# Four neighbouring rows per partition: another order of the rows of q, k and v, and of the output

## The chip, the cores and the metric

The kernel runs on one core of a Trainium2 chip. The metric is the device time of one execution in microseconds, the median of three runs. Five engines work in parallel, each through its own queue in order: PE (matrix multiply), DVE (vector), ACT (activation), POOL (GpSimd) and SP, which here issues nearly all transfers (DMAs). A time with "profile" beside it is from one further execution, recorded by the profiler.

## The reference

Attention over 8 batches of 8 heads, 576 rows and 64 columns, where each query keeps only its 32 largest scores, followed by two matrix products with a squared ReLU between them:

```
scores = (q @ k.T) / 8                      # 576 x 576 for each head
kth    = 32nd largest score of each row
scores = where(scores >= kth, scores, -1e9)
attn   = softmax(scores)
x      = (attn @ v), heads side by side     # 4608 x 512
out    = square(relu(x @ w_in)) @ w_out     # 512 -> 2048 -> 512, float32
```

## The kernel before

**The work.** Two heads form a pair, and a pair is loaded together (`load_pair`, from line 653; for the first pair `load_first`, from line 597). The 576 rows of a head are taken as four blocks of 128 and a rest of 64. The tiles `rq` and `rk` have the shape 128 x 5 x 2 x 64 (partition, block, head, column), so a partition holds the same row of both heads side by side; `rv` has 128 x 10 x 64, with the four blocks of one head after another and then the two rests. For one head of q or k one DMA brings the four blocks (line 663, 128 KB) and one the rests of both heads (line 666, 32 KB); v has two DMAs of 128 KB (line 673) and two of 16 KB (line 677). Before the change, block `tb` holds rows `128*tb` to `128*tb + 127`, so a partition's four rows lie 128 rows apart in DRAM.

PE transposes the blocks (line 585), ACT copies them into `qk` (lines 711 to 714), POOL casts v into `vb` (line 715; line 647 for the first pair). A group is one block of 128 queries of a pair: PE computes its scores against all 576 keys of both heads into PSUM (line 582), ACT copies them to `s` (line 755), DVE and POOL find the 32nd largest. For this the 576 columns are folded as four quarters of 144 (DVE line 905, POOL line 900): the largest of each four in one list, the others in three more, and then eight are taken at a time with MAX8 and MATCH_REPLACE8 (lines 934 to 946). This is right only if each list yields no more than it should; `verdict` (line 1388) tests it at the end of the kernel, and if a row failed, the whole work is done again by a second plan that runs MAX8 over all 576 columns. Four groups are searched by a threshold instead (`hunt`, with a MAX8 at line 814), and have a test of their own. ACT turns the threshold into a mask (line 965), PE transposes and masks the scores, ACT takes the exponential (line 1021), and PE multiplies by v.

**The output side.** POOL divides (line 1096), a DMA transposes `x` into `xt` (line 1109; line 1115 for the rests), and `feed` (from line 1121) runs the two matrix products over chunks of 128 or 256 rows. ACT copies each result of 128 rows to `o` (two buffers, line 1172), and SP stores it (line 1180): 128 rows of 2 KB, next to each other in the output. The last 128 rows go through `feed_last` (from line 1184), which stores two halves of 256 columns (line 1245).

**The order.** A planner (`Plan.schedule`, line 141) simulates the five queues when the kernel is built. Each operation has a duration, a priority and the tiles that it takes; the planner writes the order of each queue from that, and the order is then fixed. Where it sees PE idle it adds matmuls on `ones_bf` or `ident_bf` that compute nothing needed; ten of them stand at the start. Loads are planned by the number of their DMAs and a bandwidth figure, not by their patterns. The SP queue is in order too: a DMA that waits for its buffer holds the ones behind it. The first pair's k comes by three DMAs: one head and the rests on ACT's queue, the other head on SP's; the first block of q comes before the other three.

Of the kernel before, what the change touches and what calls it, by code (L numbers as in the profile page):

```python
# [13 lines left out]
P = 128  # L14
# [370 lines left out]
def bass_top_k_attn__then__act_relu_squared_kernel(  # L385
# [8 lines left out]
    NB, H, S, D = q.shape  # L394
# [194 lines left out]
    def build(full, weights, pl):  # L589
# [7 lines left out]
        def load_first(b, hp, rq, rq2, rk, base):  # L597

            def part(t, src, h, tb, n_):
                r0 = 128 * tb + (64 if h and src is k else 0)  # L600
                return at(t)[:, tb:tb + n_, h, :], src[b, 2 * hp + h, r0:r0 + 128 * n_, :].rearrange(
                    "(tb p) d -> p tb d", p=P)

            def rest(t, src, r0, d0):
                x = src[b, 2 * hp, r0:r0 + 64, :]
                return at(t)[0:64, 4, :, :], bass.AP(x.tensor, x.offset, [x.ap[0], [(S + d0) * D, 2], x.ap[1]])

            def start(queue, *parts):
                return lambda: [queue.dma_start(*x()) for x in parts]

            both = bass.AP(q.tensor, q[b, 2 * hp, 0:P, :].offset, [[D, P], [S * D, 2], [1, D]])
            pl.op("sp", .1, base - 82, start(nc.scalar, lambda: part(rk, k, 0, 0, 4),
                                             lambda: rest(rk, k, REST[0], REST[1] - REST[0])),
                  w=[rk], take=[rk], sem=slot_sem, ndma=2, via="act")
            pl.op("sp", 4.0, base - 81, start(nc.sync, lambda: part(rk, k, 1, 0, 4)), w=[rk], sem=lambda o: "first", ndma=1)
            pl.op("sp", 3.5, base - 80, start(nc.sync, lambda: (at(rq)[:, 0, :, :], both)), w=[rq], take=[rq],
                  sem=slot_sem, ndma=1)
            pl.op("sp", 3.5, base - 79, start(
                nc.sync, lambda: part(rq2, q, 0, 1, 3), lambda: part(rq2, q, 1, 1, 3), lambda: rest(rq2, q, 512, 0)),
                w=[rq2], take=[rq2], sem=slot_sem, ndma=3)  # L620
# [32 lines left out]
        def load_pair(b, hp, base):  # L653
            rq, rk, rv = tile("rq"), tile("rk"), tile("rv")


            def load(t, src, rest):
                def fn():
                    r = at(t)
                    res = []  # L660
                    for h in range(2):
                        r0 = 64 if h and rest != (512, 512) else 0
                        res.append(nc.sync.dma_start(r[:, 0:4, h, :], src[b, 2 * hp + h, r0:r0 + 512, :].rearrange(
                            "(tb p) d -> p tb d", p=P)))
                    x = src[b, 2 * hp, rest[0]:rest[0] + 64, :]
                    res.append(nc.sync.dma_start(r[0:64, 4, :, :], bass.AP(
                        x.tensor, x.offset, [x.ap[0], [(S + rest[1] - rest[0]) * D, 2], x.ap[1]])))
                    return res
                return fn

            def loadv():
                r = at(rv)
                res = [nc.sync.dma_start(r[:, 4 * h:4 * h + 4, :], v[b, 2 * hp + h, 64 * h:64 * h + 512, :].rearrange(
                    "(tb p) d -> p tb d", p=P)) for h in range(2)]

                for h in range(2):
                    res.append(nc.sync.dma_start(r[64 * h:64 * h + 64, 8 + h, :], v[b, 2 * hp + h, REST[h]:REST[h] + 64, :]))
                return res

            via = not full and not state["pairs"]  # L680
            state["pairs"] += 1
            if via:
                rq2 = tile("rq")
                load_first(b, hp, rq, rq2, rk, base)
            else:
                pl.op("sp", 2.3, base - 80, load(rq, q, (512, 512)), w=[rq], take=[rq], sem=slot_sem, ndma=3,
                      bw=BW * 1.9)
                pl.op("sp", 2.3, base - 79.9, load(rk, k, REST), w=[rk], take=[rk], sem=slot_sem, ndma=3, bw=BW * 1.9)
            pl.op("sp", 2.3, base - 70, loadv, w=[rv], take=[rv], sem=slot_sem, ndma=4, bw=BW * 1.9)
            qk, vb = tile("qk"), tile("vb")  # L690
            if via:
                return first_pair(rq, rq2, rk, rv, qk, vb, base)
            tq, tk, tx = Tile(psum), Tile(psum), Tile(psum)

            def t4(o, src):
                def fn():
                    for tb in range(4):
                        ins = tr(bank(o)[:, 128 * tb:128 * tb + 128], at(src)[:, tb, :, :].rearrange("p h d -> p (h d)"), ident32[:, :])
                    return ins
                return fn  # L700

            def t5():
                for i, s in enumerate((rq, rk)):
                    ins = tr(bank(tx)[:, 64 * i:64 * i + 64], at(s)[0:64, 4, :, :].rearrange("p h d -> p (h d)"), ident32[0:64, 0:64])
                return ins

            o_q = pl.op("pe", .46, base - 45, t4(tq, rq), r=[rq], w=[tq], take=[tq, qk])
            pl.op("pe", .49, base - 44.9, t4(tk, rk), r=[rk], w=[tk], take=[tk], order=[o_q])
            pl.op("pe", .22, base - 44.8, t5, r=[rq, rk], w=[tx], take=[tx], order=[o_q])

            pl.op("act", .565, base - 42.5, lambda: act.copy(at(qk)[:, 0:512], bank(tq)), r=[tq], w=[qk])  # L711
            pl.op("act", .565, base - 42.4, lambda: act.copy(at(qk)[:, 640:1152], bank(tk)), r=[tk], w=[qk])  # L712
            pl.op("act", .245, base - 42.3, lambda: act.copy(at(qk)[:, 512:640], bank(tx)[:, 0:128]), r=[tx], w=[qk])
            pl.op("act", .205, base - 42.2, lambda: act.copy(at(qk)[:, 1152:1216], bank(tx)[:, 64:128]), r=[tx], w=[qk])  # L714
            pl.op("gp", .68, base + 5, lambda: gp.tensor_copy(at(vb)[:, :, 0:D], at(rv)[:, :, :]),
                  r=[rv], w=[vb], take=[vb])
            return qk, vb
# [372 lines left out]
        def collect(got, tt, quick):  # L1090
# [27 lines left out]
                        r=[xr], w=[xt], take=[xt] if first else [], ndma=2, bw=1.0, sem=lambda o, hp=hp: f"z{xr.slot}_{hp}"))  # L1118
            return ops

        def feed(chunk, xt, tm, step):

            nt = sum(n_ for _, _, n_ in chunk)
            b = chunk[-1][0]
# [32 lines left out]
            for tb in range((nt + 127) // 128):  # L1157
                n_ = min(128, nt - 128 * tb)
                op_, ob = Tile(psum), tile("o")
                to = tm + step * (len(gs) + 1 + 4 * tb)  # L1160
                for sub in range(8):
                    def fo(sub=sub, op_=op_, tb=tb, n_=n_):
                        for fb in range(2 * sub, 2 * sub + 2):
                            c = nt * (fb % kf) + 128 * tb
                            ins = mm(bank(op_)[0:n_, :], at(gs[fb // kf])[:, c:c + n_], wo[:, fb, :], fb == 0)
                        return ins

                    pl.op("pe", .432, to + lag + step * sub / 2 - (27 if chunk is CHUNKS[-2] else 0), fo,
                          r=sorted({gs[fb // kf] for fb in range(2 * sub, 2 * sub + 2)}, key=lambda t: t.num),
                          w=[op_], take=[op_, ob] if sub == 0 else [], after=weights[8 + sub:9 + sub], order=[ho],  # L1170
                          nbf=to + step * sub / 2 if not last else 0)
                pl.op("act", .565, to + lag + 4 * step, lambda op_=op_, ob=ob, n_=n_: act.copy(  # L1172
                    at(ob)[0:n_, :], bank(op_)[0:n_, :]), r=[op_], w=[ob])
                rows, at_ = [], 0
                for b_, r0, m_ in chunk:
                    lo_, hi_ = max(at_, 128 * tb), min(at_ + m_, 128 * tb + n_)
                    if lo_ < hi_:
                        rows.append((lo_ - 128 * tb, hi_ - lo_, S * b_ + r0 + lo_ - at_))
                    at_ += m_
                pl.op("sp", 2.3, to + lag + 4 * step + 1, lambda ob=ob, rows=rows: [nc.sync.dma_start(  # L1180
                    out[row:row + m_, :], at(ob)[p0:p0 + m_, :]) for p0, m_, row in rows],
                    r=[ob], ndma=len(rows), sem=lambda o: f"o{o.tiles[0].slot}")

        def feed_last(chunk, xt, tt, turns):
# [56 lines left out]
            for e in range(2):  # L1241
# [1 line left out]
                pl.op("act", .42, tt, lambda e=e, half_=half_: act.copy(  # L1243
                    at(ob)[0:nt, half_], bank(ops[e])[0:nt, 0:256]), r=[ops[e]], w=[ob])
                pl.op("sp", 2.3, tt + e, lambda half_=half_: [nc.sync.dma_start(
                    out[S * b + q0:S * b + q0 + nt, half_], at(ob)[0:nt, half_])], r=[ob], ndma=1, sem=lambda o, e=e: f"oe{e}")

        xts = [None] * len(CHUNKS)
        turned = {}
# [276 lines left out]
```

## Time and profile before

| what | value |
|---|---|
| time, median of 3 runs | 775.21 us (775.09 to 775.52) |
| the profiled execution's own time | 774.41 us |
| its span, first to last instruction | 772.6 us |
| DVE busy | 751.6 us (97%) |
| ACT busy | 717.9 us (93%) |
| PE busy | 713.3 us (92%) |
| POOL busy | 687.6 us (89%) |
| DMA packets, bytes | 145033, 52.63 MB |
| of them under 512 B | 137088 |
| granted TensorE clock | 0.998 of full speed |

The span leaves out what lies before the first and after the last instruction; that is the difference to the execution's own time. In a line of the timeline stand the start and the duration in microseconds, the engine (PEld is PE's weight load, a name with a q at the end is the queue's sequencer, which issues DMAs), the line of the kernel, the operation, the tiles (written <- read), how many instructions, and in brackets the idle time before them and what ended it. In a list of DMA issues stand the bytes of one and the median time from issue to landing.

### The profile page before, as it was taken

Reading aid. Unit: us, or ns where it says so; the run is one execution under the profiler, and the core shown is the slowest. Engines: PE = TensorE matmul, PEld = TensorE weight load, DVE = VectorE, ACT = ScalarE, POOL = GpSimd, SP = SyncE. Lnnn points to the kernel's source line nnn. Section 1 sums busy time; section 2 is a strip of 40 time slices with the busy share of each in tenths; the row PEclk is TensorE's granted clock in tenths of the full one; section 3 lists DMA queues with packets and bytes.
Section 4 is the critical chain, followed back from the end, with each engine's and each line's share of the span. In section 5 each row is a group of like instructions: output and inputs, shape, how many; then the busy total and the mean of one; then the engine's idle time right before and its main releaser. Section 6 shows DMA issues by size and latency. Waiting matters only on the chain.

```text
span 772.6 us, 27813 instructions
## 1 busy us (share of the span) xinstructions
PE 713.3 (92%) x10680; PEld 528.2 (68%) x10680; DVE 751.6 (97%) x3589; ACT 717.9 (93%) x1141; POOL 687.6 (89%) x720
## 2 busy tenths in 40 slices
PE   7888888999989999998999889999899999999999
PEld 3656666666666676666767657686677777767776
DVE  5999999999999999999999999899999999999996
ACT  4799989899899999999999999999999999998884
POOL 4898998889789899989999899899999998989991
PEclk9999999999999999999999999999999999999999
DMA  7657452032400134103340043301332021100101
GB/s 191 182 137 196 132 135 52 23 83 48 114 11 9 51 83 95 32 16 85 70 99 10 18 111 86 69 6 46 93 82 67 11 68 38 34 23 23 36 23 34
DMA packets 145033, 52.63 MB, mean 68 GB/s; under 512 B 137088, under 2 KB 137344, under 8 KB 144896
## 3 DMA queue, kind: packets, MB, share of 16 engines
q1 hardware_dynamic: 144224, 50.66, 26.7%
q8 instruction: 84, 1.38, 0.8%
q14 instruction: 53, 0.43, 0.2%
q10 hardware_dynamic: 672, 0.16, 0.1%
HBM read 36.70 MB, written 9.44 MB: 60 GB/s over the span
## 4 chain that ended last, share of the span: by engine, by line
ACT 58%; PE 31%; DVE 8%; issue 2%; DVEq 0%; ACTq 0%
PE ps L582 26%; ACT w L965 13%; ACT p L1021 12%; ACT s L755 12%; ACT g L1140 7%; PE ps L585 5%; ACT hz L776 4%; ACT g L1155 3%; DVE f L943 2%; DVE f L905 2%; ACT o L1172 2%; DVE c L939 2%; ACT av L1087 2%; ACT qk L711 1%; ACT qk L712 1%
## 5 line engine op out<-in xcount | busy, mean ns | idle before, releaser
L900 POOL TENSOR_TENSOR f<-u,f 128x864 int32<-128x864 int32 x138 | 236.7, 1715 | 7.6
L965 ACT ACTIVATE w<-s,kth 128x576 bf16<-128x576 f32 x278 | 220.2, 829 | 3.5 <-DVE kth L946 3.5
L943 DVE MATCH_REPLACE8 f<-c,f 128x98 f32<-128x98 f32 (+2 forms) x840 | 221.2, 270 | 0.0
L939 DVE MAX8 c<-f 128x8 f32<-128x98 f32 (+2 forms) x840 | 201.5, 272 | 0.0
L582 PE MATMUL ps<-qk 64*128 64x384 f32 (+3 forms) x1280 | 179.5, 427 | 6.9 <-DVE f L905 5.8
L900 POOL TENSOR_TENSOR u<-f,s 128x576 int32<-128x576 int32 x138 | 166.5, 1206 | 16.6 <-DVE f L905 15.9
L1021 ACT ACTIVATE p<-ps 128x1152 bf16<-128x1152 f32 x144 | 169.1, 1174 | 12.5 <-PE ps L582 11.9
L755 ACT COPY s<-ps 128x1152 f32<-128x1152 f32 x140 | 162.0, 1157 | 17.3 <-PE ps L582 16.9
L582 PEld LDWEIGHTS ps<-qk 64*128 64x128 f32 (+1 forms) x1280 | 130.5, 175 | 39.6 <-DVE f L905 11.8
L582 PE MATMUL ps<-wo,g 128*128 128x512 bf16 (+1 forms) x592 | 142.9, 375 | 2.7 <-ACT qk L714 1.2
L582 PE MATMUL ps<-xt,win 128*128 128x256 bf16 (+1 forms) x1280 | 132.5, 252 | 8.5 <-ACT g L1140 3.6
L900 POOL TENSOR_TENSOR u<-s 128x288 int32<-128x288 int32 x138 | 110.2, 799 | 29.8 <-ACT s L755 26.5
L905 DVE TENSOR_TENSOR f<-ps,f 128x288 f32<-128x288 f32 x280 | 123.7, 442 | 0.1
L946 DVE MAX8 kth<-f 128x8 f32<-128x296 f32 x280 | 120.7, 456 | 0.0
L585 PEld LDWEIGHTS ps<-ident,s 64*128 64x128 f32 x2520 | 96.8, 139 | 30.9 <-ACT w L965 15.1
L582 PEld LDWEIGHTS ps<-xt,win 128*128 128x128 bf16 x1280 | 97.2, 98 | 29.3 <-ACT g L1140 6.0
L934 DVE MAX8 f<-f 128x8 f32<-128x288 f32 x280 | 114.7, 447 | 0.0
L585 PE MATMUL ps<-ident,s 64*128 64x64 f32 x2520 | 107.0, 227 | 4.6 <-ACT w L965 4.1
L1152 POOL TENSOR_TENSOR g<-g 128x512 bf16<-128x512 bf16 x86 | 89.4, 1042 | 2.9 <-ACT g L1140 2.6
L582 PEld LDWEIGHTS ps<-wo,g 128*128 128x128 bf16 x592 | 49.6, 98 | 55.2 <-issue 5.7
L1140 ACT ACTIVATE g<-ps 128x512 bf16<-128x512 f32 x140 | 86.2, 641 | 1.0 <-PE ps L582 0.9
L582 PEld LDWEIGHTS ps<-vb,p 128*128 128x128 bf16 (+1 forms) x1600 | 54.0, 100 | 32.7 <-ACT g L1140 10.5
(104 smaller groups left out, 859.1 us busy)
## 6 DMA issues: line engine op xcount, KB each, us to landing
rv<-in_v_dram SPq DMA_DIRECT2D x64, 128.0 KB, 2.4
rk<-in_k_dram SPq DMA_DIRECT2D x63, 128.0 KB, 2.5
rq<-in_q_dram SPq DMA_DIRECT2D x62, 128.0 KB, 2.5
out_dram<-o SPq DMA_DIRECT2D x31, 256.0 KB, 2.2
g<-in_moe_w_in_dram SPq DMA_DIRECT2D x8, 512.0 KB, 4.2
g<-in_moe_w_out_dram SPq DMA_DIRECT2D x8, 512.0 KB, 4.3
out_dram<-o SPq DMA_DIRECT2D x10, 128.0 KB, 2.3
rq<-in_q_dram SPq DMA_DIRECT2D x32, 32.0 KB, 2.5
```

The source lines that it names most:

```text
L582: return pe.matmul(o, l, r, start=start, stop=stop, skip_group_check=True)
L585: return pe.matmul(o, i, ident, is_transpose=True, skip_group_check=True, **kw)
L755: cp = [pl.op("act", 1.1, tg - LEAD + 1, lambda: act.copy(at(st)[:, :, 0:S], two(banks(ss)[:, FIRST_AT:], SECOND, S)), r=[ss], w=[st])]
L900: return pl.op("gp", dur, prio, lambda: gp.tensor_tensor(o().bitcast(I32), x().bitcast(I32), y().bitcast(I32), op), **kw)
L905: return dve(.36, lambda: vec.tensor_tensor(o(), two(banks(ss)[:, FIRST_AT + c:], SECOND, QUART), x(), ALU.max), r=[ss], **kw)
L934: prev[i] = [dve(.065 + HALF / 960, lambda i=i: vec.max(at(f)[:, i, A + 7:A - 1:-1], at(f)[:, i, M + QUART:E]), after=prev[i] + [low], hol ...
L939: lambda i=i, t=t, c0=c0, c1=c1: vec.max(eighth(t, i), at(f)[:, i, c0:c1]),
L943: lambda i=i, t=t, c0=c0, c1=c1: vec.match_replace(at(f)[:, i, c0:c1], eighth(t, i), at(f)[:, i, c0:c1], NEG), hold=[f])]
L946: ks.append(chain(kth, i, prev[i], .065 + (8 + HALF) / 960, lambda i=i: vec.max(eighth(kth, i), at(f)[:, i, A:M + QUART]), hold=[f]))
L965: masks[i:] = [pl.op("act", .77, tw + .8 * i, lambda i=i: act.activation(at(wt)[:, i, :], at(st)[:, i, 0:S], ACTF.Relu, bias=kth[:, i, n:n ...
L1021: return act.activation(at(pt)[:, :, :].rearrange("p c (h q) -> p h c q", h=2), bass.AP(x.tensor, x.offset, [x.ap[0], [APART, 2], [64, 9], ...
L1140: return act.activation(at(g)[:, 0:kf * nt], bank(hh)[:, 0:kf * nt], ACTF.Relu)
```

## The change

In every load of four blocks, partition p now takes rows 4p to 4p+3, which lie together in DRAM (1 KB), instead of rows p, 128+p, 256+p and 384+p. Block `tb` so holds rows 4p+tb. For the second head of a pair k and v start at row 64 as before. The first pair's first block of q takes every fourth row. The rests of 64 rows stay. The keys of a head change their order among the score columns, and v changes in the same way. The output of a block of 128 queries goes to every fourth row of the 512 (`block`), 8 KB apart instead of 2 KB. Tiles, buffers, the number of DMAs, the engines' instructions and the planner's figures are the same.

```
         def load_first(b, hp, rq, rq2, rk, base):
             def part(t, src, h, tb, n_):
-                r0 = 128 * tb + (64 if h and src is k else 0)
-                return at(t)[:, tb:tb + n_, h, :], src[b, 2 * hp + h, r0:r0 + 128 * n_, :].rearrange(
-                    "(tb p) d -> p tb d", p=P)
+                r0 = 64 if h and src is k else 0
+                return at(t)[:, tb:tb + n_, h, :], src[b, 2 * hp + h, r0:r0 + 512, :].rearrange(
+                    "(p tb) d -> p tb d", p=P)[:, tb:tb + n_, :]
...
-            both = bass.AP(q.tensor, q[b, 2 * hp, 0:P, :].offset, [[D, P], [S * D, 2], [1, D]])
+            both = bass.AP(q.tensor, q[b, 2 * hp, 0:P, :].offset, [[4 * D, P], [S * D, 2], [1, D]])
...
                         res.append(nc.sync.dma_start(r[:, 0:4, h, :], src[b, 2 * hp + h, r0:r0 + 512, :].rearrange(
-                            "(tb p) d -> p tb d", p=P)))
+                            "(p tb) d -> p tb d", p=P)))
...
                 res = [nc.sync.dma_start(r[:, 4 * h:4 * h + 4, :], v[b, 2 * hp + h, 64 * h:64 * h + 512, :].rearrange(
-                    "(tb p) d -> p tb d", p=P)) for h in range(2)]
+                    "(p tb) d -> p tb d", p=P)) for h in range(2)]
...
+        def block(b, r0, m):
+            if r0 >= 512:
+                return out[S * b + r0:S * b + r0 + m, :]
+            assert m == P and r0 % P == 0
+            return out[S * b:S * b + 512, :].rearrange("(p tb) d -> tb p d", tb=4)[r0 // P]
...
-                        rows.append((lo_ - 128 * tb, hi_ - lo_, S * b_ + r0 + lo_ - at_))
+                        rows.append((lo_ - 128 * tb, hi_ - lo_, b_, r0 + lo_ - at_))
...
-                    out[row:row + m_, :], at(ob)[p0:p0 + m_, :]) for p0, m_, row in rows],
+                    block(b_, row, m_), at(ob)[p0:p0 + m_, :]) for p0, m_, b_, row in rows],
...
-                    out[S * b + q0:S * b + q0 + nt, half_], at(ob)[0:nt, half_])], r=[ob], ndma=1, sem=lambda o, e=e: f"oe{e}")
+                    block(b, q0, nt)[:, half_], at(ob)[0:nt, half_])], r=[ob], ndma=1, sem=lambda o, e=e: f"oe{e}")
```

## The prediction

> **What bounds the kernel now.** I read the page first, then the busy time by stretches of the span, then what the DVE waited for, then which engines waited for a DMA.
>
> ```profile
> span 772.6 us, 27813 instructions
> PE 713.3 (92%) x10680; PEld 528.2 (68%) x10680; DVE 751.6 (97%) x3589; ACT 717.9 (93%) x1141; POOL 687.6 (89%) x720
> ...
> q1 hardware_dynamic: 144224, 50.66, 26.7%
> ```
> ```profile
> core 0: us, PE busy (x) PEld busy (x) DVE busy (x) ACT busy (x) POOL busy (x), PEclk, DMA share, GB/s
> 60.00:120.00 60.00, 51.79 (x771) 38.50 (x772) 60.00 (x294) 55.88 (x86) 56.08 (x51) 1.00 0.58 149
> ...
> 480.00:600.00 120.00, 114.78 (x1750) 86.39 (x1749) 116.75 (x560) 118.64 (x194) 111.71 (x118) 1.00 0.26 59
> ```
> ```profile
> DVE qk L639 <- PE ps L585: 4.6, 1, 4.6
> DVE f L905 <- ACT s L755: 3.5, 5, 2.6
> ...
> POOL vb L715 <- DMA rv<-in_v_dram: 4.9, 1, 4.9
> POOL vb L647 <- DMA rv<-in_v_dram: 1.0, 1, 1.0
> PE ps L582 <- DMA rq<-in_q_dram: 0.2, 1, 0.2
> ```
>
> The DVE is the limit: 60.00 of 60 us from 60 to 120 us, and even its weakest long stretch is 116.75 of 120. Its two largest waits are for PE and ACT, and they are mostly the start (4.6 us, and 2.6 of 3.5). The last three lines are all the waits of the whole span that the waits view puts down to a DMA: 6.1 us in three places, POOL's casts of v for the first two pairs of heads and one PE transpose. The DMA engines work 26.7% of their time for queue 1, and the change touches only DMAs. So it can move the end in four ways only: the loads before the first DVE work, the loads of the second pair of heads, a transfer so late in the steady part that an in-order engine stops for it, and the stores that end the kernel.
>
> **The start.** No instruction of PE, DVE, ACT or POOL changes: tiles, shapes and the planner's costs stay, so the order on every queue stays. What changes is when data land.
>
> ```profile
> 1.06 3.81 PE L582 MATMUL ps<-ones_bf 128*128 128x512 bf16 x10 [1.06 <-DVE ones_bf L1328]
> 1.27 2.34 SPq L609 DMA_DIRECT2D rq<-in_q_dram  x4
> ...
> 4.72 0.33 PE L585 MATMUL ps<-ident,rq 128*128 128x128 f32 x1
> ...
> 4.93 0.86 PE L585 MATMUL ps<-ident,rk 128*128 128x128 f32 x5
> ...
> 8.90 0.46 DVE L905 TENSOR_TENSOR f<-ps,s 128x288 f32<-128x288 f32 x1 [2.58 <-ACT s L755]
> ```
> ```profile
> rq<-in_q_dram SPq DMA_DIRECT2D x1, 64.0 KB, 2.8
> rk<-in_k_dram ACTq DMA_DIRECT2D x1, 32.0 KB, 3.3
> ...
> L609 ACTq DMA_DIRECT2D rk<-in_k_dram x2: 505/608/712, 0.7 to 1.3; - x2
> ```
>
> The first q block is issued at 1.27 and lands 2.8 us later, at 4.1; the last part of k is the second ACT DMA, issued at 1.3, landing 3.3 later, at 4.6. PE transposes q only at 4.72 and k at 4.93, because ten warm-up matmuls stand ahead on its queue until 4.87. So the data wait for PE, by 0.6 and 0.3 us. An earlier landing gains nothing here. A later one costs nothing up to 0.3 us of slip on the ACT queue; without that cover each further tenth goes straight into the chain to the DVE's fold at 8.90. Cost taken: 0.
>
> **What the loads become.** For v the four rows of a partition lie together on both sides, 1 KB to 1 KB. For q and k they lie together in DRAM only: the tile keeps two heads side by side (5 x 2 x 64 floats), so `r[:, 0:4, h, :]` is four pieces of 256 B at a pitch of 512 B. What a small and a 1 KB packet cost is seen in a stretch that is nearly all v loads, and in the last stores:
>
> ```profile
> q1 hardware_dynamic: 1733, 0.42, 43.3%
> ```
> ```profile
> DMA packets 292, 0.30 MB, mean 80 GB/s; under 512 B 32, under 2 KB 288, under 8 KB 288
> ...
> q1 hardware_dynamic: 288, 0.26, 21.2%
> ```
>
> The first window is 473.5 to 478 us: 4.5 x 16 engines x 43.3% = 31.2 us over 1733 packets, 18 ns each. The second is 768.9 to 772.6: 3.7 x 16 x 21.2% = 12.6 us; less 32 tiny packets at 18 ns or less, 256 packets of 1 KB at about 47 ns. A v load of 128 KB falls from 512 x 18 = 9.2 to 128 x 47 = 6.0 us of engine time, over 16 engines 0.58 to 0.38 us: it lands 0.2 us earlier, and 64 of them free 205 of 12362 engine-microseconds, 1.7 points of the 26.7%. [...] Nothing on the path gets shorter by 0.2 us on v, since only POOL's first two casts wait for it, and POOL waits for ACT afterwards (next part). [...]
>
> The other price is the issue: SP and ACT issue one DMA after another, and a q or k load now has 512 consecutive rows on one side and 128 partitions of four pieces on the other. No row of before shows that form. The nearest rows:
>
> ```profile
> L663 SPq DMA_DIRECT2D rq<-in_q_dram x62: 368/508/1542, 6.0 to 629.1; - x62
> L666 SPq DMA_DIRECT2D rq<-in_q_dram x31: 607/627/1374, 7.2 to 629.7; - x31
> ```
>
> A load over 64 partitions takes 627 ns to issue with a quarter of the bytes, so form matters more than size. Call d the extra time for one q or k load. The low end is 368 - 508, -0.14 us (the same loads at their best); the high end 1542 - 508, 1.0 us (their worst). I take 627 - 508 = 0.12, the nearest row of another form. DMAs with 0.12 more on their way still land in time above: 4.6 + 0.12 is before 4.93.
>
> **The second pair of heads** has the least room after the start.
>
> ```profile
> 9.55 0.63 SPq L666 DMA_DIRECT2D rk<-in_k_dram  x1
> ...
> 13.22 0.63 PE L585 MATMUL ps<-ident,rk 128*128 128x128 f32 x4
> ...
> 14.36 0.72 POOL L715 CAST vb<-rv 128x640 bf16<-128x640 f32 x1 [4.94 <-DMA rv<-in_v_dram]
> ...
> 14.65 0.23 ACT L714 COPY qk<-ps 128x64 f32<-128x64 f32 x1
> ...
> 15.47 1.24 PE L582 MATMUL ps<-qk 64*128 64x192 f32 x8
> ...
> 16.76 1.12 ACT L755 COPY s<-ps 128x1152 f32<-128x1152 f32 x1 [1.88 <-PE ps L582]
> ...
> 17.96 0.80 POOL L900 TENSOR_TENSOR u<-s 128x288 int32<-128x288 int32 x1 [2.88 <-ACT s L755]
> ...
> 18.92 0.45 DVE L905 TENSOR_TENSOR f<-ps,s 128x288 f32<-128x288 f32 x1
> ```
> ```profile
> DMA to landing us min/median/max: 3.5/3.5/3.5
> ```
>
> The last line is for the k load issued at 9.55: it lands at 13.1, PE uses it at 13.22, so a slip is felt at once on PE. Its copies end at 14.88, the scores that read them start at 15.47 (they wait for a DVE fold): 0.59 us of room. Then the ACT copy ends at 17.88 and the DVE folds at 18.92, being busy until then: 1.04 more. On SP five changed loads stand ahead of this landing (one k of the first pair, two q and two k of the second), so the slip is 5d = 0.6 us at d = 0.12, of 1.63. POOL's cast of v, at 14.36 for its load, may come 0.6 later and still lies in the 2.88 us that POOL then waits for ACT. Cost: 0.
>
> **The steady part.** Past the second pair no wait for a DMA is left in the list. The queue that could be late is SP's, where the transposes of x stand behind loads. A close case:
>
> ```profile
> 160.91 0.61 SPq L666 DMA_DIRECT2D rq<-in_q_dram  x1
> ...
> 161.69 1.05 POOL L1096 TENSOR_TENSOR x<-av,rzall 128x512 bf16<-128x512 f32 x1
> ...
> 162.76 1.23 SPq L1109 DMA_TRANSPOSE xt<-x  x1
> ```
>
> SP is done with four changed loads at 161.52 and then stands 1.24 us for POOL. Four times 0.12 is 0.5 us, hidden; this cover is gone at d = 0.3, and then the transpose would be late by 4d - 1.24. Cost: 0. Most stores land long before their buffer is needed, 8 KB instead of 2 KB between their rows changes no packet count; cost 0.
>
> **The end.** The final two stores are on the path.
>
> ```profile
> 768.38 0.81 SPq L1245 DMA_DIRECT2D out_dram<-o  x2
> ...
> out_dram<-o SPq DMA_DIRECT2D x1, 128.0 KB, 1.7
> ...
> out_dram<-o SPq DMA_DIRECT2D x31, 256.0 KB, 2.2
> ```
>
> They stay 128 pieces of 1 KB, farther apart. Bounds: between -0.2 (the 0.2 us by which bigger pieces move 128 KB sooner, as far down as any row goes) and 2.2 - 1.7 = +0.5; I take 0, since count and size are those of the 1.7 row.
>
> Sum: 0 + 0 + 0 + 0 on a span of 772.6. The profiled run's own time is 774.4, 1.8 over the span; the median of the timed runs is 775.2, 0.8 over that. Forecast 775.2.
>
> **The rivals.** A measurement of this kernel can tell about 0.2%, 1.55 us, from no change.
>
> *Slower, by the issue on SP.* If d is not 0.12 but large, the second pair's k comes late and the DVE stands before 18.92: cost 5d - 1.63. It decides from d = 0.33, passes 1.55 us at d = 0.64 and reaches 3.4 us, 778.6, at d = 1.0. For it: the form of these loads is new to the trace, and L666 shows that form can cost more than bytes. Against: d = 0.64 would be 1.15 us for one load, almost twice L666's median. Chance of over 0.2%: 0.09.
>
> *Slower, by the stores.* If rows 8 KB apart land like the 2.2 row the end is +0.5, 775.7; for more than 1.55 the landing would have to be 3.2 us. Chance of that 0.03.
>
> *Slower, by the second pass.* The kernel picks the 32 largest scores through folds of four quarters of the columns, tests at the end whether that held, and otherwise does everything again with plain MAX8 over 576 columns. The new order of rows of k is a new order of columns. The repeat would cost at least 144 groups x 8 MAX8 of 748 ns, 860 us (row below), so over 1630. I applied the folds and picks to the scores of the reference's seeded inputs: in the new order no row of 35840 fails, and none of the 1024 rows that are searched by threshold; of 40 random orders, 7 had a failing row. Chance 0.01.
>
> ```profile
> L814 DVE MAX8 hk<-hz x8: 715/748/764, 273.0 to 553.9; 128x8 f32<-128x576 f32 x8
> ```
>
> *Faster.* Earlier landings would have to end a wait. At the start the most is the 0.2 us by which a load lands sooner, 775.0, and the warm-up matmuls stand in front of it. More needs landings hidden in waits put down to other engines. Chance of over 0.2%: 0.04.
>
> *It does not do what it says.* For q and k the pieces stay 256 B. That gives the same time, so it lies inside the forecast; I hold it likelier than not.
>
> **How the numbers follow.** Forecast, within 0.2%: 0.83. Slower: 0.09 + 0.03 + 0.01 = 0.13. Faster: 0.04. The range goes down to 774.6 (0.2 at the start, 0.2 at the end and 0.2 of spread between runs), and up to 776.7: the 0.5 of the stores and 1.0 for d = 0.53.
>
> **What would show it.** Queue 1 should fall from 144224 packets by 64 x 384 = 24576 to about 119600 if only v has 1 KB pieces, by some 72000 if q and k have too. The median issue of L663 gives d. DVE's fold should start at 8.9, and the third group's at 18.9. A DVE wait over 1 us near 18 us, a wait of PE for rk or of POOL for v after 20 us, or a final landing over 2.2 us would prove me wrong.

## The result: 0.25% slower, and the profile after

The changed kernel takes 776.37 us (median of 13 runs, 775.66 to 779.99), beside 775.09 us (774.34 to 776.56) for the kernel before on the same chip: a ratio of 1.0025, interval 1.0016 to 1.0034. The medians alone lie 1.28 us apart (0.17%) and the means 2.10 us (0.27%): five of the thirteen changed runs, all at a granted clock of 0.996 or less, took 777.19 to 779.99 us. I had forecast no change, with 0.83 on it, and the case that I held likeliest did not come. That the time lies inside my range is luck: the range reached up to 776.7 for slower stores and a late second pair, and most of the loss came elsewhere.

The page after, the lines that answer to those of before:

```profile
span 777.2 us, 27813 instructions
PE 715.6 (92%) x10680; PEld 529.5 (68%) x10680; DVE 752.3 (97%) x3589; ACT 718.3 (92%) x1141; POOL 687.7 (88%) x720
...
q1 hardware_dynamic: 119648, 50.66, 25.3%
...
rv<-in_v_dram SPq DMA_DIRECT2D x64, 128.0 KB, 2.3
rk<-in_k_dram SPq DMA_DIRECT2D x63, 128.0 KB, 2.8
```

Instructions and their busy times are as before; only queue 1 has changed, from 144224 packets to 119648. The profiled execution is one of the long ones, 779.0 us. From the view that lists what one line issued, the median issue times (min/median/max in ns):

```profile
L663 SPq DMA_DIRECT2D rq<-in_q_dram x62: 543/622/1052, 6.5 to 633.9; - x62
...
L673 SPq DMA_DIRECT2D rv<-in_v_dram x64: 328/432/1868, 4.2 to 663.4; - x64
```

DVE runs the same 3589 instructions in the same order in both kernels, so the start of any of them after, less its start before, tells how much has been lost up to there. Read so, the 4.6 us between the two spans arise in few places: 0.87 us ahead of the first fold, 0.73 from 69 to 75 us, 1.09 from 123 to 134 us, 1.46 from 561 to 568 us, and 0.4 in small pieces. Two of these are TensorE's clock. The busy times by stretches, after and then before (the eighth figure, PEclk, is the granted clock):

```profile
67.54:70.95 3.41, 3.41 (x46) 3.14 (x43) 3.27 (x18) 1.99 (x3) 2.43 (x3) 0.50 0.36 98
562.47:565.88 3.41, 3.41 (x43) 2.43 (x44) 2.49 (x15) 2.61 (x4) 3.33 (x3) 0.50 0.57 135
```
```profile
21.12:24.53 3.41, 3.41 (x18) 2.80 (x15) 3.31 (x19) 2.01 (x3) 2.41 (x3) 0.50 0.95 252
67.54:70.95 3.41, 2.54 (x52) 2.20 (x48) 3.41 (x15) 3.36 (x5) 2.46 (x3) 1.00 0.58 145
```

The profiled execution after had two stretches of 3.41 us at half clock, at 67.54 and 562.47; the one before had one, at 21.12. Such stretches come near the same places in profiles of kernels whose later loads are the old ones (68.23 and 27.27 in one, 560.44 in another), so the 2.2 us behind these two can't be put down to the change. How often they come is another matter; *The sum*, below, returns to it.

What is left to explain is the start and the place from 123 to 134 us. The latter is where the loss is. In the kernel before (SP's timeline, POOL's, what line 1109 issued at 118.35, PE's and DVE's):

```profile
116.70 0.94 SPq L663 DMA_DIRECT2D rk<-in_k_dram  x2
117.68 0.63 SPq L666 DMA_DIRECT2D rk<-in_k_dram  x1
118.35 1.28 SPq L1109 DMA_TRANSPOSE xt<-x  x1
```
```profile
116.97 1.25 POOL L1096 TENSOR_TENSOR x<-av,rzall 128x640 bf16<-128x640 f32 x1
```
```profile
DMA to landing us min/median/max: 2.5/2.5/2.5
```
```profile
121.39 0.61 PE L582 MATMUL ps<-xt,win 128*128 128x256 bf16 x4
126.57 0.45 DVE L905 TENSOR_TENSOR f<-ps,s 128x288 f32<-128x288 f32 x1
```

And in the changed kernel, the same five views:

```profile
118.73 1.25 SPq L663 DMA_DIRECT2D rk<-in_k_dram  x2
120.02 0.63 SPq L666 DMA_DIRECT2D rk<-in_k_dram  x1
120.70 1.28 SPq L1109 DMA_TRANSPOSE xt<-x  x1
```
```profile
119.01 1.25 POOL L1096 TENSOR_TENSOR x<-av,rzall 128x640 bf16<-128x640 f32 x1
```
```profile
DMA to landing us min/median/max: 4.5/4.5/4.5
```
```profile
125.28 0.60 PE L582 MATMUL ps<-xt,win 128*128 128x256 bf16 x4 [1.70 <-issue]
129.32 0.46 DVE L905 TENSOR_TENSOR f<-ps,s 128x288 f32<-128x288 f32 x1 [0.63 <-ACT s L755]
```

Before, x is written at 118.22 and its transpose issued at 118.35, as soon as SP has done with the k loads of the eleventh pair (pair no. 10); it lands 2.5 us later and PE finds it there. After, x is written at 120.25, SP is still at the k loads until 120.65, the transpose is issued at 120.70, and it takes 4.5 us. PE stands 1.70 us ("issue": for nothing that the view can name), and DVE stands for ACT's copy behind it. While the transpose is on its way, a packet of queue 8 starts, 16 KB of instructions (the page has 84 of this queue, 1.38 MB). A window of 0.1 us from 122.6 in the changed kernel, and one of 0.3 us from 120.7 in the kernel before, show it:

```profile
q8 instruction: 1, 0.02, 92.4%
```
```profile
q8 instruction: 1, 0.02, 29.2%
```

The view counts a packet whole in the window in which it starts: 92.4% of 0.1 us x 16 engines is 1.48 us for this packet; before it is 1.40. In the changed kernel this packet starts 1.92 us behind the issue of the transpose, before the change 2.36 us, when it is all but landed at 2.5. So there were three suspects: longer issue in sum, the late transpose by itself, and the packet.

### The profile page after: what moved, and what is told of

It is laid out like the page before. It is cut to its first block, busy times and chain, and to the rows that moved or that the text cites. A ratio compares the mean times of both kernels' runs of the same rounds, so it can differ in the third digit from the quotient of the medians.

```text
span 777.2 us, 27813 instructions
## 1 busy us (share of the span) xinstructions
PE 715.6 (92%) x10680; PEld 529.5 (68%) x10680; DVE 752.3 (97%) x3589; ACT 718.3 (92%) x1141; POOL 687.7 (88%) x720
## 3 DMA queue, kind: packets, MB, share of 16 engines
q1 hardware_dynamic: 119648, 50.66, 25.3%
q8 instruction: 84, 1.38, 0.7%
## 4 chain that ended last, share of the span: by engine, by line
ACT 57%; PE 26%; DVE 12%; POOL 3%; issue 2%; DVEq 0%; POOLq 0%; ACTq 0%
PE ps L582 22%; ACT w L965 13%; ACT p L1021 12%; ACT s L755 11%; ACT g L1146 6%; PE ps L585 5%; ACT hz L776 4%; DVE f L943 3%; DVE f L905 3%; ACT g L1161 3%; DVE c L939 2%; ACT av L1087 1%; ACT o L1178 1%; DVE kth L946 1%; ACT qk L711 1%
```

## The experiments

All ratios are to the kernel before, run on the same chip at the same time, five rounds each. "Loss" is what DVE loses from 123 to 134 us against the profile before.

**Which part of the change.** Four kernels have one part each.

```
e1_stores: only block() and the two stores     e2_first: only part() and both in load_first
e3_qk:     only line 663                       e4_v:     only line 673
```

> Only the stores take the new form (rows of the output 8 KB apart); all loads are as before, so the rows of the output stand in another order. Theory 'start' (the loss lies in the first pair's loads) and theory 'issue' (it lies in the later q and k loads, which take longer to issue): within 0.2 us of before. Theory 'stores': +0.2 us from the last landing (1.91 against 1.74 us in the two profiles), and up to +1 if the stores in the middle count. Theory 'clock' (the loss is stretches of half TensorE clock, whose place differs from run to run): runs with a granted clock of 1.000 are within 0.2 us of such runs of before, runs under 1.000 are 1 to 4 us longer.

> Only the first pair's loads of q and k take the new form; all else is as before (so the first pair's queries and its v stand in another order than they should). Theory 'start': +0.6 to +1.2 us, with the first q block landing near 4.85 instead of 4.1 us and the DVE's first fold at 9.1 or later instead of 8.9. Theory 'issue': at most +0.3. Theory 'stores': 0. Theory 'clock': as before within 0.2 us at a granted clock of 1.000, and the first fold moves with the moment at which the clock rises (4.05 us in the profile of before, 6.10 in that of the changed kernel), not with the loads.

> Only the later pairs' loads of q and k take the new form (their v and the output's rows keep the old order, so the result is another). Theory 'start': 0 within 0.2 us. Theory 'issue': +0.6 to +1.2 us; median issue of these loads 0.62 instead of 0.51 us, the second pair's k landing 0.5 us later and the third group's scores and fold later than 15.47 and 18.92 by up to that. Theory 'stores': 0. Theory 'clock': 0 at a granted clock of 1.000.

> Only the later and first pairs' loads of v take the new form, the one that has 1 KB pieces on both sides (v then stands in another order than the keys, so the result is another). All theories: between -0.2 and 0 us; 24576 packets fewer on queue 1, v's landing 0.1 to 0.2 us earlier, issue 0.43 instead of 0.51 us. Theory 'clock': the spread between runs stays as it is in before.

Measured: stores 0.9997 (0.9986 to 1.0008), first pair 1.0004 (0.9995 to 1.0012), later q and k 1.0028 (1.0017 to 1.0040), v 0.9997 (0.9988 to 1.0006). Only the later q and k loads show a loss, about 2.2 us by the ratio and more than the 0.6 to 1.2 I had expected; for the others the runs can tell none. Theory 'clock' alone falls: the three runs of the q and k kernel at full clock take 776.60 us at the median, the 19 of the kernel before 775.49. In the run of q and k alone:

```profile
124.40 0.60 PE L582 MATMUL ps<-xt,win 128*128 128x256 bf16 x4 [1.50 <-issue]
```

It has the same hole at the same matmul (loss 0.89 us), and the runs with stores, first pair or v have none there (0.00 to within 0.01).

**One pair, or all.** The changed kernel with pair no. 10's k and v in the old row order:

```
+            own = state["pairs"] == ONE                       # ONE = 10
-                            "(p tb) d -> p tb d", p=P)))      # q, k
+                            "(tb p) d -> p tb d" if own and src is k else "(p tb) d -> p tb d", p=P)))
-                    "(p tb) d -> p tb d", p=P)) for h in range(2)]            # v
+                    "(tb p) d -> p tb d" if own else "(p tb) d -> p tb d", p=P)) for h in range(2)]
```

> The changed kernel, with one pair put back: the k and v loads of pair no. 10 (the eleventh pair to be loaded, some 116 to 119 us into the span) take row 128 tb + p again, both of them so that keys and values still agree. Theory 'one place': the two head loads of k of that pair stand directly ahead of the transposes of the expert's input on SP, and delay them by about 0.3 us, which puts them under a 16 KB instruction-fetch packet; there they take 4.3 to 4.5 us instead of 2.5 to 2.6, and TensorE, then VectorE, stand for about 0.9 us (offset of VectorE 0.50 at 127.7 plus 0.37 at 133.2). Expected then: these transposes land 2.4 to 2.7 us after issue, no idle time of over 0.5 us ahead of the L582 matmul that reads xt near 125 us, and a ratio to the kernel before of 1.0005 to 1.0015 (775.6 to 776.3 beside a kernel before at 775.2), down from 1.0025. Rival 'spread issue': the loss comes in small amounts from all 60 loads; one pair of them gives back under 0.1 us, ratio 1.002 to 1.003. Rival 'chance fetch': the fetch packet falls on these transposes in any case; landing stays at 4 us or more, ratio 1.002 to 1.003.

Measured: 775.86 us beside 775.29, 1.0005 (0.9994 to 1.0017). The transpose lands in 2.55 us, PE doesn't stand, the loss is 0.00. One pair of 31 gives back the loss; "spread issue" falls. "Chance fetch" falls too: the packet started 2.37 us behind the issue again.

**The issue time alone.** The kernel before, row order untouched; a switch keeps some loads off the short way of issuing a DMA.

```
e6_one_slow:  nc.dge_precook = not (own and src is k)   # before the loop over the two heads, True again behind it
e7_all_slow:  nc.dge_precook = False                    # for all later q and k loads of 128 KB
```

> The kernel before with its row order unchanged everywhere; a switch of the library keeps the two head loads and the rest load of k of pair no. 10 alone off the short way of issuing a DMA, so that their issue takes longer (0.54 to 0.65 us each by the rows of the changed kernel, instead of 0.37 to 0.51). No data moves otherwise. Theory 'one place': the transposes of the expert's input behind them are issued 0.3 us or more later, fall under the instruction packet and land after 4 us or more; TensorE stands ahead of the xt matmul near 125 us, VectorE loses 0.5 to 0.9 us there, ratio to before 1.0006 to 1.0015. Rival 'spread issue': three longer issues of about 110 are worth under 0.05 us, ratio 0.9995 to 1.0004. Rival 'data pattern' (the 256-byte reads of every fourth row themselves slow the memory or the queue for what follows): row order is as before, so nothing changes, same ratio.

> The kernel before with its row order unchanged; all q and k loads after the first pair are kept off the short way of issuing, so each takes 0.54 to 0.65 us on SP instead of 0.37 to 0.51. Theory 'issue' (in sum or at one place): like the run with only the later q and k loads in the new order, ratio 1.002 to 1.004, with idle time of TensorE ahead of the xt matmul near 125 us and the second pair's folds about 0.3 us later. Theory 'one place' expects no more of it than 0.2 us above the run with one pair slow plus the 0.3 us of the second pair. Rival 'data pattern': the reads of every fourth row are what costs, so ratio 0.9995 to 1.0005 here.

The two loads of pair no. 10 in the first, and PE at its matmul:

```profile
L665 SPq DMA_DIRECT2D rk<-in_k_dram x2: 640/646/651, 117.4 to 118.0; - x2
```
```profile
123.84 0.60 PE L583 MATMUL ps<-xt,win 128*128 128x256 bf16 x4 [1.65 <-issue]
```

Two loads with a longer issue (the rest load kept its 0.64) bring the ratio to 1.0028 (1.0015 to 1.0041), more than I expected of it and no less than all the later q and k loads in the new order; the loss is 1.04 us. All of them slow gives 1.0015 (1.0002 to 1.0028), loss 1.23: nothing on top that the runs can tell. No row of q, k or v was read in another order here, so the data pattern is out. How long SP takes to issue is what matters, and at one place.

**The start.** The changed kernel with pair no. 10 put back and the first two DMAs of SP's queue exchanged (q block ahead of head 2 of k):

```
+    main.order["sp"][i], main.order["sp"][j] = sp[1], sp[0]
```

> The changed kernel with pair no. 10's k and v in the old row order and, besides, the first two DMAs of SP's queue exchanged: the first q block ahead of head 2 of the first k. The start: in the changed kernel the q block is issued behind k's longer issue and lands about 1 us later than before, which moved TensorE's first transposes from 4.72 to 5.2 us at equal clock and the end by 0.3 to 0.5 us. With q first its landing comes 0.5 to 0.7 us earlier and k head 2 about 0.5 us later; k's transposes stood at 4.93 and follow q's. If q's landing is what sets the start, the first fold comes 0.2 to 0.3 us earlier at an equal clock and the ratio to before falls to 1.000 to 1.001; if k head 2 takes over as the last to land, the start stays where it is or slips by up to 0.3 us and the ratio is that of the run with one pair put back, or up to 0.0004 above it. This is also the candidate for a version as fast as the kernel before; none of the theories expects it to be faster by more than 0.0005.

Measured 1.0003 (0.9990 to 1.0015): with the other run's 1.0005, no difference that can be told. What the traces say of the start is below.

**The packet.** Queue 8 has 84 packets in the page, and PE issues 10680 matmuls and 10680 weight loads: 254 for a packet, if all of them are PE's, as an estimate; in the trace before, 256 matmuls and weight loads start between one packet and the next, at the median. More PE instructions ahead should then move the packet forward against PE's work; the runs below, with 12 to 80 more, moved it by 1.0 to 5.0 us. So the warm-up matmuls, which compute nothing needed, can move it and leave loads, stores and SP's order as they are.

```
e9_fetch_away (changed kernel), e12_before_away (kernel before): ten of 512 columns become fifty of 103
e10_fetch_onto (kernel before): five of the ten become four each of 128
e11_order (changed kernel): k of pair no. 10 behind the transposes on SP; first q block ahead of k head 2
```

> The changed kernel, all loads and stores new; only the ten warm-up matmuls of 512 columns at the start become fifty of 103 columns, 515 columns of output instead of 512 for each. TensorE's instruction stream is fetched in packets of 16 KB, one for about 256 matmuls and weight loads; eighty more of these ahead make every later packet come about eighty such instructions, some 3 us, earlier against TensorE's work. Theory 'fetch': the packet that fell 1.9 us behind the issue of the transposes of x (122.62 against 120.70) falls before that issue; they land 2.3 to 2.6 us after issue instead of 4.5, TensorE doesn't stand ahead of the xt matmul, VectorE doesn't lose the 0.7 and 0.37 us there, and the ratio to before falls from 1.0025 to 1.0003 to 1.0012, although the k loads' longer issue is still there. Rival 'delay alone': the 0.3 us by which SP issues the transposes late is what costs; landing may be short, but VectorE still loses 0.3 to 0.5 us there and the ratio stays at 1.0015 or above. Rival 'queue': the landing of over 4 us comes from the reads of k ahead of the transposes in the same queue; nothing changes, ratio 1.002 to 1.003.

> The kernel before with the fifty shorter warm-up matmuls: the control for the run of the changed kernel with them. Theory 'fetch': in the kernel before no transpose on the path crosses a packet, so moving the packets by 3 us gains nothing, unless another transpose with little room comes under one: ratio 0.9995 to 1.0005, start within 0.1 us of before at an equal clock. If fifty short matmuls cost time at the start themselves, up to 0.5 us more, which is then to be taken off the other run too.

> The kernel before, loads and stores untouched; five of the ten warm-up matmuls become four of 128 columns each, so fifteen matmuls and fifteen weight loads more, and TensorE's instruction packets come about 0.5 us earlier against its work. In the kernel before the packet near 120.7 us starts 2.37 us behind the issue of the transposes of x, just before they land. Theory 'fetch': it now starts 1.7 to 2.1 us behind it, the transposes land 3.8 to 4.3 us after issue instead of 2.5, TensorE stands 1 us or more ahead of the xt matmul, VectorE loses 0.5 to 1.1 us near 126 to 133, ratio 1.0006 to 1.0020, with no load changed. Rivals 'delay alone' and 'queue': SP issues everything as before, so the landing stays at 2.5 and the ratio at 0.9995 to 1.0005.

> The changed kernel, all loads and stores new, with two changes of order on SP alone: the three k loads of pair no. 10 go behind the transposes of x instead of ahead of them (TensorE reads that k 35 us later), and the first q block goes ahead of head 2 of the first k. All theories but 'queue by the data pattern' expect the transposes to be issued when x is written, 2.3 us or more ahead of the instruction packet, to land 2.4 to 2.7 us after issue, and the ratio to be that of the run with one pair put back, 1.000 to 1.001. The packet starts so close behind that landing that a slip of 0.1 us would bring the long landing back: then 1.001 to 1.002.

With the whole change and the packet moved away (SP, then the landing, then PE):

```profile
117.57 1.82 SPq L663 DMA_DIRECT2D rk<-in_k_dram  x2
119.43 0.63 SPq L666 DMA_DIRECT2D rk<-in_k_dram  x1
120.11 1.28 SPq L1109 DMA_TRANSPOSE xt<-x  x1
```
```profile
DMA to landing us min/median/max: 2.6/2.6/2.6
```
```profile
122.77 0.60 PE L582 MATMUL ps<-xt,win 128*128 128x256 bf16 x4 [0.35 <-PE ps L582]
```

The ratio falls to 1.0005 (0.9995 to 1.0016), the loss to 0.00. x was written at 119.09, so SP issued its transpose 1.02 us late, later than in the changed kernel itself (0.45), and nothing was lost: "delay alone" falls. Most of this lateness isn't the new row order's: the two k loads took 1.82 us to issue instead of 1.25, now that the packet runs beside them. The control has the same (1.77 instead of 0.94, the transpose 0.96 us late), lost 0.00 too, and has 1.0002 (0.9991 to 1.0013). Another order on SP, all loads new, does it too: issued 0.03 us behind x, landed after 2.46, loss 0.00, 1.0001 (0.9990 to 1.0011). So the change can be had without a loss that the runs can tell, in this form or the other; no form of it beat the kernel before.

The packet meant to be put onto the transposes went too far: 30 PE instructions moved it by 2.1 us instead of 0.5, to 0.26 us behind the issue. There the landing grew to 3.42 us with SP as before, against "delay alone" and "queue", but it was borne: loss 0.00, 0.9998 (0.9987 to 1.0010). So two more, with six and with ten of the warm-up matmuls cut into two of 256 columns:

> The kernel before, loads, stores and SP untouched; six of the ten warm-up matmuls are cut into two of 256 columns, so six matmuls and six weight loads more, and TensorE's packets come a few tenths of a us earlier against its work (thirty more moved this one by 2.1 us). Theory 'packet': if the packet near 121 us starts 1.0 to 2.2 us behind the issue of the transposes of x, they take 3.5 to 4.3 us instead of 2.5, TensorE stands 0.5 us or more ahead of the xt matmul and VectorE loses 0.3 to 1.0 us at 126 to 134; ratio 1.0004 to 1.0015. Rival 'late issue needed as well': a landing of up to 4.3 us is borne, since the issue is as early as before; no loss, ratio 0.9995 to 1.0004. If the packet starts 2.3 us or more behind the issue, neither is tested and nothing changes.

> The same with all ten warm-up matmuls cut into two of 256 columns, ten matmuls and ten weight loads more: the packet a few tenths of a us earlier still, between the run with six and the run with fifteen. The theories expect of it what they expect of the run with six, by where the packet starts behind the issue of the transposes: 0.3 to 1.0 us behind, landing of 3.2 to 3.6 us and no loss; 1.0 to 2.2 us behind, landing of 3.5 to 4.3 us and by 'packet' a loss of 0.3 to 1.0 us.

The packet now started 1.32 and 1.34 us behind the issue. With ten cut (POOL; SP; the landing; the packet in the window from 118.7 to 120.1; PE):

```profile
117.33 1.26 POOL L1096 TENSOR_TENSOR x<-av,rzall 128x640 bf16<-128x640 f32 x1
```
```profile
118.70 1.28 SPq L1109 DMA_TRANSPOSE xt<-x  x1
```
```profile
DMA to landing us min/median/max: 4.4/4.4/4.4
```
```profile
q8 instruction: 1, 0.02, 6.9%
```
```profile
123.15 0.60 PE L582 MATMUL ps<-xt,win 128*128 128x256 bf16 x4 [1.24 <-issue]
```

Every load, every store and SP are those of the kernel before, the transpose is issued 0.11 us behind x (0.14 there), and the hole is there: loss 0.63 us, ratio 1.0016 (1.0001 to 1.0031). So "late issue needed as well" falls. With six cut the transpose took 3.90 us, loss 0.18, less than the 0.3 to 1.0 expected, ratio 1.0005 (0.9993 to 1.0017). That the two landings differ by 0.46 us, with the packet at the same place, may come from the packet's own time, 1.21 and 1.55 us; no run shows it. All at this one place, times in us:

| kernel | issue behind x written | packet behind issue | issue to landing | x written to landing | loss |
|---|---|---|---|---|---|
| order changed (e11) | 0.03 | 2.89 | 2.46 | 2.49 | 0.00 |
| before | 0.14 | 2.36 | 2.51 | 2.65 | 0 |
| one pair put back (e5) | 0.14 | 2.37 | 2.55 | 2.69 | 0.00 |
| before, 30 more (e10) | 0.11 | 0.26 | 3.42 | 3.53 | 0.00 |
| changed, packet away (e9) | 1.02 | 2.88 ahead | 2.57 | 3.59 | 0.00 |
| before, packet away (e12) | 0.96 | 2.65 ahead | 2.59 | 3.56 | 0.00 |
| before, 12 more (e13) | 0.11 | 1.32 | 3.90 | 4.01 | 0.18 |
| before, 20 more (e14) | 0.11 | 1.34 | 4.36 | 4.47 | 0.63 |
| later q, k only (e3) | 0.44 | 2.25 | 4.29 | 4.73 | 0.89 |
| one pair slow (e6) | 0.54 | 2.31 | 4.34 | 4.88 | 1.04 |
| changed | 0.45 | 1.92 | 4.49 | 4.94 | 1.09 |
| all slow (e7) | 0.53 | 1.97 | 4.54 | 5.07 | 1.23 |

In the six rows with a loss it is the fifth column less 3.84 us, to within 0.01, and no row under 3.84 loses anything: that one number, fitted to these rows, is the cover that the place has. A late issue or a packet, each alone, can stay under it (a packet alone can also pass it, by 0.63 us); the new loads' 0.3 us brings the transpose from just ahead of the packet (2.36 us, landing 2.51) under it (2.31 or less, landing 4.3), and goes over it by 1.09.

## Why the prediction was wrong, step by step

*The loads.* Right. q and k keep their 256 B pieces and only v gets 1 KB: 119648 packets, against 119600. v lands 0.1 us sooner at the median of the page (2.4 to 2.3), k and q later (2.5 to 2.8 and 2.7). "It does not do what it says", for q and k, held, as I thought likelier than not.

*The issue.* d = 622 - 508 = 0.11 us against 0.12 taken. Right, though the cause I had for it, form and not bytes, was only argued; v's loads, with one run of 1 KB on both sides, went the other way, 508 to 432.

*The steady part.* This step failed. I took one "close case", the transpose at 162.76 where SP stands 1.24 us for POOL, for the closest, and looked among those with a wait to spare. The tight one has no wait in the list at all: at 118.35 the transpose is issued 0.14 us behind its input, and what delays it is SP's own k loads, an engine busy and not waiting. Three loads stand ahead of it, two of them changed, so 2d was 0.31 us there (0.94 to 1.25 for the two). By the cover of 3.84 us alone that would still have been hidden: 2.65 + 0.31 = 2.96. What I did not have is that the landing itself would grow from 2.5 to 4.5. So the step was "cost 0" for this place, and the runs put 1.09 us in its stead in the profile. The rival "slower, by the issue on SP" named the right engine, but the wrong place, the second pair, and a price 5d - 1.63 that starts at d = 0.33; the loss came at d = 0.11. None of the signs that I had named as proof against me came; they watched the second pair, waits for rk and v, and the end, not this place.

*The second pair.* Right for the change as a whole: third fold less first, 19.79 - 9.77, is the 10.02 us of before. The k load landed at 14.42 instead of 13.09, a slip of 1.33 us where I had counted 0.6, but under the 1.63 of room; PE, itself 0.87 later, stood 0.45 us for it, and DVE did not feel that. (The time from first to third fold isn't the same in every run: 10.25 in the one with only the later q and k loads, 10.25 too in the one with only the first pair, 10.38 in the kernel before with thirty more PE instructions. So the extra 0.2 to 0.4 us can't be put down to the loads alone, and its cause stays open.)

```profile
9.77 0.46 DVE L905 TENSOR_TENSOR f<-ps,s 128x288 f32<-128x288 f32 x1 [2.58 <-ACT s L755]
```
```profile
19.79 0.44 DVE L905 TENSOR_TENSOR f<-ps,s 128x288 f32<-128x288 f32 x1
```

*The start.* Partly wrong. The first q block is issued at 1.51 instead of 1.27 and lands at 4.85 instead of 4.08, a slip of 0.8 us where I had counted d; the cover, until 4.72, is gone. In the profile after, that cost nothing, because PE's warm-up matmuls ran longer that time; the run with only the later q and k loads, whose first loads are the old ones, had the same rows (4.02, 1.49 and 5.30):

```profile
4.03 1.49 PE L582 MATMUL ps<-ones_bf 128*128 128x512 bf16 x3
5.31 0.42 PE L585 MATMUL ps<-ident,rq 128*128 128x128 f32 x1
```

Where the warm-up went fast, as in the run with only the first pair new, it shows:

```profile
3.60 1.28 PE L582 MATMUL ps<-ones_bf 128*128 128x512 bf16 x4
5.18 0.30 PE L585 MATMUL ps<-ident,rq 128*128 128x128 f32 x1 [0.31 <-PE ps L582]
```

PE transposes q at 5.18 instead of 4.72, and the first fold starts at 9.23 instead of 8.90. So 0.33 us in this execution, in which the clock was up at 4.06 us and q landed at 5.09; the timed runs of that kernel (1.0004, 0.9995 to 1.0012) can't confirm it. With the q block first on SP (e8) it landed at 2.75, and PE took it up at 5.14 straight behind the warm-up; but the clock was up only at 4.94 there, so its first fold, at 9.32, doesn't tell what that order is worth.

*The stores.* Taken as 0; the traces show about 0.2 us, inside my bounds. In the six traces with the new stores the last one lands after 1.91 to 2.01 us, in the ten others after 1.74 to 1.83. The runs can't tell it (0.9997).

*The sum.* The ratio 1.0025 is 1.9 us (1.2 to 2.6), of which the place explains 1.09, the last store about 0.2 and the start 0 to 0.33. The rest goes with half-clock stretches. The eight changed runs at full clock have a mean of 776.15 us, 1.03 above the mean of the kernel before (775.12, clocks not on record), about what the place costs; the five others bring the rest. That these came by chance alone is unlikely. By the profiles a mean clock of 0.998 means one such stretch and 0.996 two. Clocks of 0.996 or less were granted in 21 of 61 timed runs of the five kernels that lose 0.6 us or more at the place, and in 23 of 246 runs of all others. The nine stretches in the 16 traces that fall before the end each follow 3.41 us in which PE was busy for only 51 to 65% of the time, and the hole makes one more such stretch of low load. PE's busy time is the third figure: after, ahead of the half clock at 67.54 and across the hole, and before, at the same place of the work:

```profile
64.13:67.54 3.41, 1.99 (x38) 1.11 (x32) 3.41 (x16) 3.41 (x6) 3.41 (x4) 1.00 0.32 94
121.90:125.31 3.41, 1.71 (x42) 1.19 (x40) 3.35 (x13) 2.54 (x3) 2.83 (x3) 1.00 0.24 49
```
```profile
119.86:123.27 3.41, 2.90 (x67) 2.22 (x65) 3.41 (x14) 2.54 (x3) 2.83 (x3) 1.00 0.20 39
```

So the hole may bring half clock of its own in some executions, by 50% against 85%. That is not shown: no trace has such a stretch behind the hole, and the kernel with six matmuls cut, whose PE was busy for 77% there, had five such runs of twelve.

## What to carry to other kernels

A change that lengthens the issue of a DMA can be paid by what stands behind it in the same queue (here two k loads, 0.31 us longer to issue in sum, ahead of a transpose whose place lost 1.09 us), so look for transfers that follow a changed one without a gap; a list of waits doesn't name them, since the queue is busy and not waiting. For each of those take the time from input written to landing and set it against the use, and expect the landing itself to be no constant (2.5 to 4.5 us here): ask what else crosses it. Where one such place costs, reorder that queue there; here k stood ahead of the transposes though PE read it only 36 us after it landed (156.05 against 120.06 in the kernel before).

## What the runs showed of the hardware

The transposes here were slow when a 16 KB packet of instructions (queue 8) started while they were on their way. Over all 16 traces, those of xt with a packet starting 1.0 to 2.2 us behind their issue took 3.92 us at the median (74 of 624, 3.27 to 4.55), and those with none from 0.5 us ahead to 2.4 us behind it (418) took 2.44. The same places return from trace to trace, so these are fewer than 74 independent cases. Nor is the packet the only cause: 39 of the 418 took over 3 us, among them the one near 95 us in 14 of the traces. At the place studied the edge lies between 2.31 us (landing after 4.3) and 2.36 (2.5); elsewhere three packets 2.22 to 2.27 us behind the issue met landings of 2.3 to 2.4. Why a transpose lands later then, no run took apart: the packets near this place took 0.93 to 1.55 us, while the landing grew by up to 2.0 us, and by 1.8 with packets of 0.93, so a packet's own time doesn't cover all of it.

How far some PE instructions move a packet isn't a fixed time for each: 12 and 20 more moved this one by 1.0 us against the issue of the transposes and 30 by 2.1, where I had expected a few tenths and 0.5; 80 moved it by 4.8 and 5.0, where I had expected some 3.
